# Later gating and full-height angle and magnitude matmuls in a two-layer convolution kernel

## The chip, the core and the metric

The kernel runs on one core of a Trainium2 chip. The metric is the device time of one execution in microseconds (us); the time before is the median of three executions. Engines are named as in the profile: PE (TensorE matmul), PEld (its weight load), DVE (VectorE), ACT (ScalarE), POOL (GpSimd), SP (the queue that issues most DMAs).

## The reference

Four residual layers run over a sequence of 2048 rows and 512 channels, A, B, A, B:

```
x = x + A(layernorm(x), k, v, shift_k, ssm_k, ssm_D)     # twice
x = x + B(layernorm(x), ...)                             # twice, in turn with A
A(q):  kv = shortconv4(k, shift_k) * v                   # "gating"
       y  = irfft(rfft(kv) * rfft(ssm_k)) + kv * ssm_D   # long causal convolution by FFT
       return q * y
B(u):  K[d, l] = 2 * Re sum_n C[d,n] * dt[d] * exp(A[d,n] * dt[d] * l)    # 128 modes n per channel
       return irfft(rfft(u) * rfft(K)) + u * D_skip
```

The convolution in A doesn't depend on x, so it is done once for both A layers. The taps K of layer B are made from angles (the imaginary part of A·dt times l) and magnitudes (the real part).

## The kernel before

**Stages.** A prologue works out angles and magnitudes per mode (L373 to L424, mostly DVE) and writes them, each split into a high and a low part, to the DRAM tensors `rows_d` (`split`, L359). Then two Python generators are interleaved by `run_steps`, one step of `stream` to two of `diagonal`, after four steps of `diagonal` alone. A scheduler then settles the order of instructions on each engine; every engine runs its own list strictly in order.

**`stream`** makes the taps of layer B in 65 steps (16 groups of modes, four quarters each) and, as quarters of the taps are done, their spectra. For a group, `load_rows` reads the rows back (`raw`), and one DVE cast makes `rw` of them. Its matmuls are `mags` (`pm`, L479, six per group) and `angles` (`pa`, L494, four per group, each followed by a full-height matmul `pa<-y,minus`, L499). Each group holds two halves h of 64 partitions, and each of these matmuls contracts over the 64 partitions of one half. DVE and POOL then multiply sines, cosines and magnitudes to `xye` (L517 to L519, L521), and PE contracts them (`pk`, L531).

**`diagonal`** first makes the spectra of layer A's kernel, 48 steps: per quarter four steps that load a group (`kk`), add a diagonal term on POOL (L239), transform it (`pf`, L171) and transpose it (`x`, L189), then eight steps of the second transform (`pu`, L196), the copy (`pc`) and the store (`spec`). Beside them runs the **gating** (`gated`, L622): per group of channels one load (`kvt`, 624 KB), four products on POOL (`term`, L629), a copy on ACT, three sums and a product on DVE (`acc`, `un`, L637, L639) and a store (`kv_d`). 16 groups, three generator steps each. After the spectra comes A's **convolution** (59 steps) with its loads `kab`, products `sw` and `vv`, the inverse transforms `pi` and `po` and the stores `ya_d`.

**Afterwards**, with other PSUM pools, come the first layer A's update (`gated_update`, which reads `ya_d` as `yaq`), layer B's convolution, and the second pair of layers.

Gating borrows buffers: `kvt` those of `kab`, its products those of `vv` and `sw`, its sum one of the PSUM banks of `pu`.

Of the kernel before, what the change touches and what calls it, by code (L numbers as in the profile page):

```python
# [9 lines left out]
F32 = mybir.dt.float32  # L10
F32R = mybir.dt.float32r
# [9 lines left out]
NQ = 4  # L21
CK = 4
NCH = 32 // CK
# [76 lines left out]
def kernel(ctx: ExitStack, tc: tile.TileContext, out, x_in, kv_in, ssmk_in, ssmd_in,  # L100
                           la_in, ai_in, cr_in, ci_in, ldt_in, ldtb_in, dsk_in,
                           w1_in, w2_in, mm_in, w4_in, minus_in, tt_in, tg1_in, tg2_in, dbg=None):
    nc = tc.nc
    V, S, G, T = nc.vector, nc.scalar, nc.gpsimd, nc.tensor

    def sbuf(stack, name, side="left"):
        return stack.enter_context(tc.tile_pool(name=name, bufs=1, side=side, reuse_waits="tile"))

    def after(ins, first):
        tc.add_manual_dep(ins.ins, first.ins.name,  # L110
                          mybir.DependencyInfo(mybir.DependencyClass.NoSync, mybir.DependencyReason.DATA),
                          reason="activation tables")

    dram = ctx.enter_context(tc.tile_pool(name="dram", bufs=1, space=DRAM))
# [1 line left out]
    kdram = [dram.tile([128, 512], F32, name=f"kdram{g}") for g in range(16)]  # L116
    ya_d = dram.tile([4, 128, 16, 128], F32, name="ya_d")
    kv_d = [dram.tile([128, 512], F32, name=f"kv_d{g}") for g in range(16)]
    rows_d = [dram.tile([NQ, 128, 4, 128], F32, name=f"rows_d{k}") for k in range(2)]

    cpool = sbuf(ctx, "cpool")
    GL = 2
# [295 lines left out]
    tabs = {}  # L418
# [15 lines left out]
    def stage_banks(n, wide):  # L434
        sctx.close()
        pool = sctx.enter_context(tc.tile_pool(name=f"ps{n}{wide}", bufs=1, space=PSUM, reuse_waits="tile"))
        psum["c1"] = (pool, n)
        psum.pop("f1", None)
        if wide:
            psum["f1"] = (pool, wide)  # L440
# [4 lines left out]
    wk = sbuf(gctx, "wk")  # L445
# [11 lines left out]
        factors.append(xye)  # L457


    rows, ms, pks, angs = {}, {}, {}, {}  # L460
    NM = 5
    last_exp, last_sin = [None], [None]

    def load_rows(gi):
        if gi in rows:
            return
        raw = wk.tile([128, 2, 128], F32, name="raw", tag="raw", bufs=2)
        q, g = divmod(gi, 4)
        for k in range(2):
            nc.sync.dma_start(raw[:, k, :], rows_d[k][q, :, g, :])  # L470
        rows[gi] = wk.tile([128, 2, 128], F32R, name="rw", tag="rw", bufs=2)
        V.tensor_copy(rows[gi], raw)

    def mags(gi, k, col):
        h, s = divmod(k, 2)
        hs = slice(64 * h, 64 * h + 64)
        pm = pp.tile([128, 512], F32, name="pm", tag="pa", bufs=NPA)
        rhs = tabs["tg2"][hs] if col == 2 else tabs["tg1"][hs, 8 * s:8 * s + 8, :]
        mt = T.matmul(pm, rows[gi][hs, 1, :], rhs, start=True, stop=True)  # L479
        if col == 2:  # L480
            ms[gi, h] = wk.tile([128, 16, 96], F32, name="m", tag="m", bufs=NM)
            m = ms[gi, h][:, :, 64:96]
        else:
            m = ms[gi, h][:, 8 * s:8 * s + 8, 0:64]
        i = S.activation(m, pm.rearrange("p (c i) -> p c i", c=16 if col == 2 else 8), AF.Exp)  # L485
        if last_sin[0] is not None:
            after(i, last_sin[0])
        last_exp[0] = i

    def angles(gi, k):  # L490
        h, s = divmod(k, 2)
        hs = slice(64 * h, 64 * h + 64)
        pa = pp.tile([128, 512], F32, name="pa", tag="pa", bufs=NPA)
        T.matmul(pa, rows[gi][hs, 0, :], tabs["tt"][hs, 8 * s:8 * s + 8, :], start=True, stop=False,  # L494
                 skip_group_check=True)

        y = wk.tile([128, 512], F32R, name="y", tag="y", bufs=2)
        V.tensor_scalar(y, pa, MAGIC, MAGIC, op0=ALU.add, op1=ALU.subtract)
        T.matmul(pa, minus, y, start=False, stop=True, skip_group_check=True)  # L499
        angs[gi, k] = pa  # L500
# [106 lines left out]
    def z_of_a():  # L607
        turns_z[0] += 1
        return zx[:, turns_z[0] % 2].rearrange("p (x k r) -> p x k r", k=32, r=2)

    with ExitStack() as actx:
        ap = sbuf(actx, "conv_a", "right")
        zlast = []
        ZA = 2
        NSA = 2
        NKA = 3
        ADA = 1000
        LAGA = 2
        AHA = 2
        NWA = 1  # L620

        def gated(grp):  # L622
            kvt = ap.tile([128, 39, 32], F32, name="kvt", tag="kab", bufs=NKA)
            nc.sync.dma_start(kvt.rearrange("p t c -> p (t c)"), kv_in[grp])
            tap = lambda j: kvt[:, 35 + j, :][:, None, :].to_broadcast([128, 16, 32])
            terms = []
            for j, tag in enumerate(("vv", "sw", "vv", "sw")):
                term = ap.tile([128, 16, 32], F32, name="term", tag=tag, bufs=NSA)
                G.tensor_mul(term, kvt[:, 3 - j:19 - j, :], tap(j))  # L629
                terms.append(term)  # L630
                if j == 1:
                    yield
            yield
            acc = bank("acc").rearrange("p (t c) -> p t c", c=32)
            S.copy(acc, terms[0])  # L635
            for term in terms[1:]:
                V.tensor_add(acc, acc, term)  # L637
            un = ap.tile([128, 16, 32], F32, name="un", tag="pc", bufs=2)
            V.tensor_mul(un, acc, kvt[:, 19:35, :])  # L639
            nc.sync.dma_start(kv_d[grp], un.rearrange("p t c -> p (t c)"))  # L640
            yield

        KV0 = 1
        def row_stats(t):
            xt = ap.tile([128, 512], F32, name="xt", tag="kk", bufs=3)
            nc.sync.dma_start(xt, x_in[:, t, :])
            V.bn_stats(st0[:, t, :], xt)

        def kv_steps():
            for grp in range(KV0, 16):  # L650
                yield from gated(grp)

        def steps_a(q):
            z, us = {}, {}
            nop = lambda: None

            def load(g):
                us[g] = ap.tile([128, 16, 32], F32, name="u", tag="kk", bufs=3)
                nc.sync.dma_start(us[g].rearrange("p t c -> p (t c)"), kv_d[4 * q + g])

            def fwd(g):
                if g == 0:
                    z[0] = z_of_a()
                u = us[g]
                fwd_group(lambda ps_, j, n: u[ps_, :, j:j + n], z[0], 32 * g, 32, 32 if "f1" in psum else 16, zlast[4 + q - ZA], full="f1" not in psum)
                if g < 3:
                    load(g + 1)
            turns = [lambda g=g: fwd(g) for g in range(4)]
            if LAGA > 2:
                turns = [nop, turns[0], turns[1], lambda: (turns_last[0](), turns_last[1]())]  # L670
                turns_last = [lambda: fwd(2), lambda: fwd(3)]
            return (lambda: z[0]), [nop] * 7 + [lambda: load(0)] + [nop] * 4 + turns

        def finish_a(q, g, po):
            ya = ap.tile([128, 512], F32, name="ya", tag="pc", bufs=2)
            S.copy(ya, po.rearrange("p t c -> p (t c)"))
            nc.sync.dma_start(ya_d[:, :, 4 * q + g].rearrange("k p x -> p k x"), ya.rearrange("p (k x) -> p k x", k=4))

        def diagonal():
            kvs = kv_steps()  # L680
            for q in range(NQ):
                for i, _ in enumerate(spectrum_quarter(0, q, ssmk_in, ap, zlast, ZA, "c1")):
                    if q == 0 and i == 1:
                        for grp in range(KV0):
                            for _ in gated(grp):
                                pass
                    if q == 0 and i < 4:
                        nc.sync.dma_start(w2[:, 8 * i:8 * i + 8], w2_in[:, 8 * i:8 * i + 8])
                    if q == 2 and i < 4:
                        ins = nc.sync.dma_start(mm[:, 8 * i:8 * i + 8], mm_in[:, 8 * i:8 * i + 8])  # L690
                        after(ins, zlast[0])
                    if q == 3 and i == 0:
                        after(nc.sync.dma_start(w4, w4_in), zlast[0])
                    next(kvs, 0)
                    if q == 3 or q == 2 and i >= 8:
                        row_stats(12 * (q - 2) + i - 8)
                    yield
            for _ in kvs:
                yield
            stage_banks(4, 0)  # L700
            yield from convolution(0, {"conv": ap}, steps_a, finish_a, lag=LAGA, ahead=AHA, nk=NKA, ns=NSA, nw=NWA, inplace=True,
                                   add_dve=ADA, zlast=zlast)

        RT = 1
        RD = 2
        diag = diagonal()
        for _ in range(4):
            next(diag)
        run_steps([(stream(), RT), (diag, RD)])
# [254 lines left out]
```

## Time and profile before

| what | value |
|---|---|
| median of three executions | 742.3 us (741.83, 742.3, 750.0) |
| the profiled execution's own time | 734.99 us |
| its span in the profile | 733.2 us |
| mean granted TensorE clock | 0.933 |
| PE busy | 593.9 us (81%) |
| DVE busy | 531.1 us (72%) |
| ACT busy | 486.0 us (66%) |
| POOL busy | 454.8 us (62%) |

"Busy" counts the time in which an engine runs an instruction, waits apart. The span is from the first to the last instruction. The granted clock is the share of the TensorE clock that was passed; a matmul at 0.50 takes about twice as long.

### The profile page before, as it was taken

The page shows a single profiled execution, that of the slowest core. Times are in us where ns is not written, and L with a number is a line of the kernel's source. Part 1 is how long each engine was busy: PE and PEld are TensorE (multiplying, and loading weights), DVE is VectorE, ACT ScalarE, POOL GpSimd, SP SyncE. Part 2 cuts the span into 40 slices and gives each one's busy share as a digit, 9 for nine tenths or more (in the row PEclk, how much of TensorE's full clock was granted, in tenths as well). Part 3 has the DMA queues.
Part 4 walks back from the last instruction along what each step waited for, and adds up shares of the span by engine and source line. Part 5 has one row for each costly group of instructions (what it writes and reads, how often), then busy time and mean ns, then how long its engine had stood idle before and what let it go on. Part 6 is the DMA issues. An engine that isn't in the chain of part 4 may idle for free. (4 is left out here: it accounts for less than half of the span.)

```text
span 733.2 us, 14282 instructions
## 1 busy us (share of the span) xinstructions
PE 593.9 (81%) x4984; PEld 409.9 (56%) x4984; DVE 531.1 (72%) x961; ACT 486.0 (66%) x882; POOL 454.8 (62%) x473
## 2 busy tenths in 40 slices
PE   1378877698989999969998865899798817799996
PEld 0154554456766776736765454767476503476773
DVE  7857959877385785584574877376597998978775
ACT  4246566577678777776798749677655447768672
POOL 5847969678268595684596620157576612479693
PEclk9997979768999999989999996999999978899999
DMA  9769767774745457636457493567866360178682
GB/s 324 258 227 315 255 209 235 226 249 158 223 125 143 130 127 204 167 107 173 118 149 212 136 335 150 170 181 203 226 192 164 85 172 0 51 209 238 195 244 100
DMA packets 80683, 135.39 MB, mean 185 GB/s; under 512 B 8540, under 2 KB 29412, under 8 KB 79460
## 3 DMA queue, kind: packets, MB, share of 16 engines
q1 hardware_dynamic: 79716, 132.06, 60.3%
q0 software_dynamic: 896, 2.43, 1.2%
q8 instruction: 39, 0.64, 0.4%
q14 instruction: 32, 0.26, 0.1%
HBM read 98.80 MB, written 35.65 MB: 183 GB/s over the span
## 5 line engine op out<-in xcount | busy, mean ns | idle before, releaser
L285 POOL TENSOR_TENSOR sw<-sw,kab 128x512 f32<-128x512 f32 x96 | 124.9, 1305 | 66.3 <-ACT sw L282 61.3
L283 DVE TENSOR_TENSOR vv<-pu,kab 128x512 f32<-128x512 f32 x96 | 65.1, 680 | 64.1 <-ACT sw L282 44.1
L295 PE MATMUL pi<-vv,mm 128*128 128x128 f32 x768 | 105.7, 281 | 6.7 <-DVE vv L283 4.3
L286 POOL TENSOR_TENSOR vv<-vv,sw 128x512 f32<-128x512 f32 x76 | 98.6, 1301 | 14.5 <-DVE vv L283 12.0
L295 PEld LDWEIGHTS pi<-vv,mm 128*128 128x128 f32 x768 | 94.2, 193 | 20.6 <-issue 10.4
L281 ACT ACTIVATE sw<-pu 64x512 f32<-64x512 f32 x96 | 57.1, 595 | 65.7 <-PE pu L196 61.8
L171 PE MATMUL pf<-kk,wz 128*128 128x256 f32 (+1 forms) x176 | 64.7, 624 | 42.1 <-issue 15.2
L517 POOL TENSOR_TENSOR xye<-co,m 128x512 f32<-128x512 f32 x64 | 76.0, 1187 | 36.5 <-ACT co L507 12.5
L629 POOL TENSOR_TENSOR term<-kvt 128x512 f32<-128x512 f32 x64 | 81.5, 1292 | 19.5 <-ACT acc L635 9.8
L196 PEld LDWEIGHTS pu<-zu,w 128*128 128x128 f32 x512 | 63.0, 191 | 42.8 <-DVE vv L283 16.1
L196 PE MATMUL pu<-x,w 128*128 128x128 f32 x512 | 79.6, 302 | 5.9 <-ACT pc L247 2.5
L196 PEld LDWEIGHTS pu<-x,w 128*128 128x128 f32 x512 | 70.7, 209 | 21.9 <-issue 7.5
L196 PE MATMUL pu<-zu,w 128*128 128x128 f32 x512 | 72.8, 284 | 10.7 <-DVE vv L283 9.6
L171 PE MATMUL pf<-u,wz 128*128 128x256 f32 (+2 forms) x280 | 76.4, 485 | 3.0 <-DVE zu L189 1.2
L247 ACT COPY pc<-pu 128x512 f32<-128x512 f32 x64 | 37.2, 587 | 45.3 <-PE pu L196 22.6
L485 ACT ACTIVATE m<-pm 128x512 f32<-128x512 f32 x96 | 53.4, 607 | 18.5 <-PE pm L479 15.1
L316 PE MATMUL po<-w,w 128*64 128x512 f32 x192 | 53.9, 637 | 13.8 <-DVE w L310 12.0
L171 PEld LDWEIGHTS pf<-kk,wz 128*128 128x128 f32 (+1 forms) x176 | 30.1, 222 | 58.2 <-issue 29.3
L505 ACT ACTIVATE co<-pa 128x512 f32<-128x512 f32 x64 | 38.4, 600 | 30.2 <-PE pa L499 29.8
L282 ACT COPY sw<-pu 64x512 f32<-64x512 f32 x96 | 55.5, 578 | 1.1
L518 DVE TENSOR_TENSOR xye<-pa,m 128x512 f32<-128x512 f32 x64 | 43.7, 683 | 13.8 <-ACT pa L506 7.3
L479 PE MATMUL pm<-tg,rw 64*128 64x512 f32 x96 | 43.7, 517 | 10.5 <-DVE xye L519 8.3
(137 smaller groups left out, 1147.3 us busy)
## 6 DMA issues: line engine op xcount, KB each, us to landing
kab<-spec SPq DMA_DIRECT2D x188, 256.0 KB, 4.3
spec<-pc SPq DMA_DIRECT2D x64, 256.0 KB, 2.3
kvt<-kv_in SPq DMA_DIRECT2D x16, 624.0 KB, 5.3
yaq<-ya_d SPq DMA_DIRECT2D x5, 1024.0 KB, 7.5
kk<-ssmk_in SPq DMA_DIRECT2D x16, 256.0 KB, 5.1
kv_d<-un SPq DMA_DIRECT2D x16, 256.0 KB, 4.1
xt<-x_in SPq DMA_DIRECT2D x16, 256.0 KB, 2.9
kdram<-ks SPq DMA_DIRECT2D x64, 64.0 KB, 2.9
```

Source lines behind the costliest of these rows:

```text
L171: yield T.matmul(o, w, rhs, start=True, stop=True)
L196: ins = T.matmul(pu[:, i, :], w2[:, c * CK + i, :], z[:, :, c * CK + i, :], start=True, stop=True)
L281: S.mul(sw[0:64], pu[64:128], -1.0)
L282: swapped[0] = S.copy(sw[64:128], pu[0:64])
L283: V.tensor_mul(vv, pu, kabs[s][:, 0])
L285: (V if last else G).tensor_mul(sw, sw, kabs[s][:, 1])
L286: (V if last or s % add_dve == add_dve - 1 else G).tensor_add(vv, vv, sw)
L295: i1s[t] = T.matmul(pi[:, i, :], mm[:, c * CK + i, :], vvs[t][:, i, :], start=True, stop=True)
L316: ins = T.matmul(po[64 * a:64 * a + 64], w4, ws[g][:, :, 16 * a:16 * a + 16, :].rearrange("p x t r -> p t x r"), start=True, stop=True, ti ...
L485: i = S.activation(m, pm.rearrange("p (c i) -> p c i", c=16 if col == 2 else 8), AF.Exp)
L517: G.tensor_mul(xye[:, 0, :, 32:96], co[:, :, 1:65], m[:, :, 32:96])
L629: G.tensor_mul(term, kvt[:, 3 - j:19 - j, :], tap(j))
```

## The change

Three things are done.

1. The first group's gating, which ran as a block at the second step of the spectra, goes the way of the other 15; and the gating generator is first stepped at the fourth step of the spectra (`KS = 3`) in place of the first. Its 48 steps then don't fit in the spectra, and the last three run beside the first seven steps of A's convolution.
2. `raw` becomes two fixed tiles of twice the width, [128, 2, 2, 128], zeroed once on POOL: half h of the modes stands in its own 64 partitions of slot h, the other 64 partitions of the slot stay zero. The cast to `rw` covers 128x512 elements in place of 128x256.
3. `mags` and `angles` contract over all 128 partitions of a slot; the table operand is taken whole.

```diff
+    raws = []
+    for i in range(2):
+        raw = wk.tile([128, 2, 2, 128], F32, name=f"raw{i}")
+        for h in range(2):
+            G.memset(raw[64 - 64 * h:128 - 64 * h, h], 0.0)
+        raws.append(raw)
...
-        raw = wk.tile([128, 2, 128], F32, name="raw", tag="raw", bufs=2)
+        raw = raws[gi % 2]
-        for k in range(2):
-            nc.sync.dma_start(raw[:, k, :], rows_d[k][q, :, g, :])
+        for h in range(2):
+            hs = slice(64 * h, 64 * h + 64)
+            nc.sync.dma_start(raw[hs, h], rows_d[:, q, hs, g, :].rearrange("k p n -> p k n"))
...
-        rhs = tabs["tg2"][hs] if col == 2 else tabs["tg1"][hs, 8 * s:8 * s + 8, :]
-        mt = T.matmul(pm, rows[gi][hs, 1, :], rhs, start=True, stop=True)
+        rhs = tabs["tg2"] if col == 2 else tabs["tg1"][:, 8 * s:8 * s + 8, :]
+        T.matmul(pm, rows[gi][:, h, 1, :], rhs, start=True, stop=True)
...
-        T.matmul(pa, rows[gi][hs, 0, :], tabs["tt"][hs, 8 * s:8 * s + 8, :], start=True, stop=False,
+        T.matmul(pa, rows[gi][:, h, 0, :], tabs["tt"][:, 8 * s:8 * s + 8, :], start=True, stop=False,
...
-        KV0 = 1
+        KV0 = 0
+        KS = 3
...
-                    if q == 0 and i == 1:
-                        for grp in range(KV0):
-                            for _ in gated(grp):
-                                pass
...
-                    next(kvs, 0)
+                    if 12 * q + i >= KS:
+                        next(kvs, 0)
...
+            for _ in range(NCH - 1):
+                next(kvs, 0)
+                next(main)
+                yield
```

What the scheduler makes of it moves instructions on every engine up to the first update. Three places at the start of the program show the pattern.

POOL, from the split of the magnitudes (`hl<-la`) on, before. `kk` is the addition for one group of the spectra, four of them make a quarter; `term` is a gating product:

```order
L363 TENSOR_TENSOR hl<-la,hl 128x512
L239 TENSOR_TENSOR kk<-kk,dr 1x32
L629 TENSOR_TENSOR term<-kvt 128x512 x2
L239 TENSOR_TENSOR kk<-kk,dr 1x32
L363 TENSOR_TENSOR hl<-ai,hl 128x512
L629 TENSOR_TENSOR term<-kvt 128x512 x2
L239 TENSOR_TENSOR kk<-kk,dr 1x32
L629 TENSOR_TENSOR term<-kvt 128x512 x7
L239 TENSOR_TENSOR kk<-kk,dr 1x32
L629 TENSOR_TENSOR term<-kvt 128x512
```

The same place with the change:

```order
L363 TENSOR_TENSOR hl<-la,hl 128x512
L239 TENSOR_TENSOR kk<-kk,dr 1x32 x3
L363 TENSOR_TENSOR hl<-ai,hl 128x512
L634 TENSOR_TENSOR term<-kvt 128x512 x4
L239 TENSOR_TENSOR kk<-kk,dr 1x32
```

The fourth `kk` stood behind eleven products and now stands behind four. Counted up to the first `xye` of the taps, POOL's list held 26 products and now holds 18.

SP, from the last two stores of `rows_d` to the first read of `raw`, before:

```order
L364 DMA rows_d_99<-hl 8x16x1024
L640 DMA kv_d_82<-un 128x512
L624 DMA kvt<-kv_in 128x1248
L229 DMA kk<-ssmk_in 128x512
L640 DMA kv_d_83<-un 128x512
L624 DMA kvt<-kv_in 128x1248
L226 DMA dr<-ssmd_in 1x128
L470 DMA raw<-rows_d_98 128x128
```

With the change:

```order
L364 DMA rows_d<-hl 8x16x1024 x2
L229 DMA kk<-ssmk_in 128x512
L226 DMA dr<-ssmd_in 1x128
L477 DMA raw_234<-rows_d 64x2x128 x2
L477 DMA raw_237<-rows_d 64x2x128 x2
```

Two stores of gating results and two loads of gating inputs no longer stand between.

DVE, from the last product of the prologue to the first casts, before:

```order
L363 TENSOR_TENSOR hl<-t_143,hl 128x512
L189 STREAM_TRANSPOSE x<-pf 128x512 x2
L637 TENSOR_TENSOR acc<-acc,term 128x512 x5
L639 TENSOR_TENSOR un<-acc,kvt 128x512
L637 TENSOR_TENSOR acc<-acc,term 128x512
L189 STREAM_TRANSPOSE x<-pf 128x512 x2
L639 TENSOR_TENSOR un<-acc,kvt 128x512
L189 STREAM_TRANSPOSE x<-pf 128x512 x2
L637 TENSOR_TENSOR acc<-acc,term 128x512
L472 CAST rw<-raw 128x256 x2
```

With the change:

```order
L363 TENSOR_TENSOR hl<-t_142,hl 128x512
L189 STREAM_TRANSPOSE x<-pf 128x512 x6
L479 CAST rw<-raw_234 128x512
L479 CAST rw<-raw_237 128x512
L642 TENSOR_TENSOR acc<-acc,term 128x512 x3
L644 TENSOR_TENSOR un<-acc,kvt 128x512
```

The casts now stand behind six transposes alone; the gating's sums come after them.

More of the change, by code (lines that the diff above doesn't have):

```diff
@@ L118 @@
     kv_d = [dram.tile([128, 512], F32, name=f"kv_d{g}") for g in range(16)]
-    rows_d = [dram.tile([NQ, 128, 4, 128], F32, name=f"rows_d{k}") for k in range(2)]
+    rows_d = dram.tile([2, NQ, 128, 4, 128], F32, name="rows_d")
     cpool = sbuf(ctx, "cpool")
@@ L466, in load_rows @@
             return
-        raw = wk.tile([128, 2, 128], F32, name="raw", tag="raw", bufs=2)
+        raw = raws[gi % 2]
         q, g = divmod(gi, 4)
-        for k in range(2):
-            nc.sync.dma_start(raw[:, k, :], rows_d[k][q, :, g, :])
-        rows[gi] = wk.tile([128, 2, 128], F32R, name="rw", tag="rw", bufs=2)
+        for h in range(2):
+            hs = slice(64 * h, 64 * h + 64)
+            nc.sync.dma_start(raw[hs, h], rows_d[:, q, hs, g, :].rearrange("k p n -> p k n"))
+        rows[gi] = wk.tile([128, 2, 2, 128], F32R, name="rw", tag="rw", bufs=2)
         V.tensor_copy(rows[gi], raw)
@@ L475, in mags @@
         h, s = divmod(k, 2)
-        hs = slice(64 * h, 64 * h + 64)
         pm = pp.tile([128, 512], F32, name="pm", tag="pa", bufs=NPA)
-        rhs = tabs["tg2"][hs] if col == 2 else tabs["tg1"][hs, 8 * s:8 * s + 8, :]
-        mt = T.matmul(pm, rows[gi][hs, 1, :], rhs, start=True, stop=True)
+        rhs = tabs["tg2"] if col == 2 else tabs["tg1"][:, 8 * s:8 * s + 8, :]
+        T.matmul(pm, rows[gi][:, h, 1, :], rhs, start=True, stop=True)
         if col == 2:
@@ L491, in angles @@
         h, s = divmod(k, 2)
-        hs = slice(64 * h, 64 * h + 64)
         pa = pp.tile([128, 512], F32, name="pa", tag="pa", bufs=NPA)
-        T.matmul(pa, rows[gi][hs, 0, :], tabs["tt"][hs, 8 * s:8 * s + 8, :], start=True, stop=False,
+        T.matmul(pa, rows[gi][:, h, 0, :], tabs["tt"][:, 8 * s:8 * s + 8, :], start=True, stop=False,
                  skip_group_check=True)
@@ L697, in diagonal @@
                     yield
+            stage_banks(4, 0)
+            main = convolution(0, {"conv": ap}, steps_a, finish_a, lag=LAGA, ahead=AHA, nk=NKA, ns=NSA, nw=NWA, inplace=True,
+                               add_dve=ADA, zlast=zlast)
+            for _ in range(NCH - 1):
+                next(kvs, 0)
+                next(main)
+                yield
             for _ in kvs:
                 yield
-            stage_banks(4, 0)
-            yield from convolution(0, {"conv": ap}, steps_a, finish_a, lag=LAGA, ahead=AHA, nk=NKA, ns=NSA, nw=NWA, inplace=True,
-                                   add_dve=ADA, zlast=zlast)
+            yield from main
         RT = 1
```

## The prediction

> **What bounds the kernel now.** I first read the page's parts 1 and 2 (PE busiest at 81%, its granted clock low in places), then cut the span into stages: prologue, spectra of A beside the first taps, A's convolution beside the other taps, and the rest. The view of windows gives busy time per engine (instruction counts in brackets), granted clock, DMA share and GB/s:
>
> ```profile
> 0.00:40.00 40.00, 11.37 (x20) 3.89 (x21) 30.65 (x45) 12.47 (x19) 25.77 (x36) 1.00 0.84 298
> 40.00:195.00 155.00, 128.64 (x1229) 82.92 (x1229) 115.20 (x214) 98.31 (x172) 112.66 (x121) 0.85 0.71 231
> 195.00:430.00 235.00, 211.70 (x2259) 150.69 (x2257) 156.06 (x249) 177.94 (x307) 156.13 (x160) 0.99 0.56 157
> 430.00:733.00 303.00, 242.14 (x1480) 172.43 (x1480) 229.15 (x454) 197.31 (x384) 160.27 (x156) 0.93 0.59 167
> ```
>
> The columns are PE, PEld, DVE, ACT, POOL. PE has little to do in the first 40 us. From 195 to 430 it is busy 90% at full clock: that stage is PE's, and what starts it earlier ends it earlier. From 40 to 195 no engine is full (PE 83%, DVE 74%, POOL 73%), but PE's clock is 0.85. After 430 the order of instructions is as good as unchanged, so I forecast no change there.
>
> In the prologue, timelines of POOL, PE and SP show one chain for the spectra and one for the taps. The rows give start, length, engine, line, and in brackets the idle time ahead and what ended it:
>
> ```profile
> 20.42 3.38 POOL L629 TENSOR_TENSOR term<-kvt 128x512 f32<-128x512 f32 x2
> ...
> 26.74 8.71 POOL L629 TENSOR_TENSOR term<-kvt 128x512 f32<-128x512 f32 x7 [2.29 <-ACT acc L635]
> 35.41 0.24 POOL L239 TENSOR_TENSOR kk<-kk,dr 1x32 f32<-1x32 f32 x1
> ```
> ```profile
> 35.70 2.07 PE L171 MATMUL pf<-kk,wz 64*128 64x512 f32 x2
> 39.19 3.78 PE L196 MATMUL pu<-x,w 128*128 128x128 f32 x16 [1.41 <-DVE x L189]
> ...
> 44.11 1.60 PE L479 MATMUL pm<-tg,rw 64*128 64x512 f32 x3
> ```
> ```profile
> 26.41 1.25 SPq L364 DMA_DIRECT2D rows_d<-hl  x2
> ...
> 34.47 0.38 SPq L640 DMA_DIRECT2D kv_d<-un  x1
> ...
> 35.98 3.63 SPq L470 DMA_DIRECT2D raw<-rows_d  x4
> ```
>
> The fourth `kk` of the first quarter runs on POOL only at 35.41, after the gating products ahead of it; `pf` follows at once, and the first `pu` at 39.19. The rows of angles and magnitudes are handed to DRAM at 26.41 to 27.66, but their read is issued at 35.98, behind a gating store that waited for its data until 34.47; the first `pm` starts at 44.11.
>
> The second thing to see is the clock. The first seven rows are the stretches at 0.50 up to 195 us and the stretch ahead of the longest; the last two are a later one, when PE ran nothing but `pf` of 128 rows, half of whose weights (`wz`) are zeros:
>
> ```profile
> 55.15:58.56 3.41, 3.41 (x13) 0.50 1.05 292
> 68.80:75.63 6.83, 6.83 (x48) 0.50 0.89 313
> 96.11:106.35 10.24, 9.32 (x57) 0.50 0.68 223
> 130.24:133.66 3.42, 3.42 (x10) 0.50 0.37 101
> 140.48:147.31 6.83, 3.53 (x39) 0.50 0.82 258
> 154.14:171.21 17.07, 16.24 (x102) 0.50 0.53 169
> 150.73:154.14 3.41, 3.33 (x38) 1.00 0.91 325
> 454.51:457.92 3.41, 1.59 (x8) 1.00 0.62 222
> 457.92:461.33 3.41, 2.32 (x11) 1.00 0.25 88
> ```
> ```profile
> 152.17 1.89 PE L479 MATMUL pm<-tg,rw 64*128 64x512 f32 x4
> 154.58 1.76 PE L494 MATMUL pa<-tt,rw 64*128 64x512 f32 x3 [0.51 <-ACT m L485]
> ```
> ```profile
> 453.91 2.19 PE L171 MATMUL pf<-kk,wz 128*128 128x256 f32 x8
> ```
>
> Low stretches last multiples of 3.41 us. The 3.41 us before the longest were busy for 3.33, much of it with `pm` of 64 rows, and the clock fell; 3.41 us that were busy for 1.59, with 128 rows of which half are zeros, were followed by 3.41 us at full clock. So busy time alone doesn't keep the clock: matmuls over 64 rows count less, and zeros in the array count. The six stretches are 47.8 us with 42.8 us of PE work, of which half, 21 us, is lost to the clock.
>
> **The change part by part**, against the profiled execution's own 734.99 us (span 733.2), which is 7.3 under the median of the timed runs, 742.3; I take the change in microseconds over to that median.
>
> *Earlier start.* In POOL's list of before the split of the angles stands right ahead of the products at 20.42; in the new one it is followed by four products and the fourth `kk`. Four products at the 3.38 for two of the row are 6.8: `kk` at 27.2 in place of 35.41, so 8.2 earlier. For the taps: only a small load stands between the stores of the rows and their read. The two stores are 1 MB; at the 298 GB/s of the first stage that is 3.5 us, so they land near 31.2 to 31.6, and the read goes 4.4 earlier. The cast also loses its place behind the gating's sums on DVE:
>
> ```profile
> 42.65 0.70 DVE L637 TENSOR_TENSOR acc<-acc,term 128x512 f32<-128x512 f32 x1 [3.52 <-POOL kk L239]
> 43.26 2.07 DVE L472 CAST rw<-raw 128x256 fp32r<-128x256 f32 x2
> ```
>
> ```profile
> raw<-rows_d SPq DMA_DIRECT2D x32, 64.0 KB, 1.9
> ```
>
> The data were there by 41.5 (last read issued by 39.61, 1.9 to land by the page's row of DMA issues), the cast ran at 43.26: 1.8 more, 6.2 together. Between 8.2 and 6.2 I take **-7**. The ends are -8.2 and 0 (if the four products wait as long for the gating inputs, which are now issued later).
>
> *Displaced gating.* Eight products fewer before the first `xye` must be done later:
>
> ```profile
> L629 POOL TENSOR_TENSOR term<-kvt 128x512 f32<-128x512 f32 x64 | 81.5, 1292 | 19.5 <-ACT acc L635 9.8 <-DVE acc L637 7.1 <-DMA kvt<-kv_in 2.3
> ```
>
> Eight by 1.29 are 10.3 us of POOL. Four of them go past the spectra, where PE is the bound and POOL busy 66%: 0. The other four, 5.2 us, fall into 40 to 195, where POOL is busy 73%; I take half, **+2.6**. The ends are 0 and +10.3. Behind a product wait its sum on ACT and DVE and, since the sum holds one of two PSUM banks, the next `pu`.
>
> *The clock.* With 128 rows, the stretch before 154.14 counts in full, and the clock should hold there; PE then saves half of 16.24, 8.1 us. But the others are near their own limits there:
>
> ```profile
> 150.00:160.00 10.00, 9.09 (x58) 5.58 (x57) 7.96 (x13) 6.67 (x14) 8.65 (x8) 0.71 0.76 251
> 160.00:170.00 10.00, 10.00 (x57) 6.08 (x56) 7.39 (x14) 6.64 (x12) 8.21 (x11) 0.50 0.49 166
> 170.00:180.00 10.00, 8.47 (x126) 6.46 (x129) 6.66 (x13) 8.69 (x16) 8.14 (x10) 0.94 0.59 193
> ```
>
> POOL has 5.0 us free in these 30, so at most that much can be had before it is the bound: **-4**. The other five stretches begin after PE stood idle, which 128 rows don't cure; some would end one step of 3.41 sooner. I put 0 on them. The ends for the whole are 0 and -10.5 (all of the 21 us lost, half of it on the path).
>
> [...]
>
> *Length of the matmuls themselves.* Rows of 64 and 128 of the same 512 columns:
>
> ```profile
> L479 PE MATMUL pm<-tg,rw 64*128 64x512 f32 x96 | 43.7, 517 | 10.5 <-DVE xye L519 8.3 <-ACT m L485 1.7
> L499 PE MATMUL pa<-y,minus 128*128 128x512 f32 x64 | 31.2, 514 | 1.2 <-DVE y L498 0.8
> ```
>
> A full one (514 ns) is no longer than a half one. But two halves can run beside each other:
>
> ```profile
> 148.76 0.73 PE L479 MATMUL pm<-tg,rw 64*128 64x512 f32 x2
> ...
> 108.14 0.98 PE L479 MATMUL pm<-tg,rw 64*128 64x512 f32 x2
> ```
>
> Two took 0.73 in one place, 0.98 in another. If the 0.25 is overlap of opposite halves and it is lost at each of at most 32 changes of half (two per group), it is 8 us of PE; as few rows show it, and part lies where PE waits, I take **+1**, with ends 0 and +8.
>
> [...]
>
> *Casts, memsets, reads.* The 16 casts double in width; a cast of 512 elements took 0.41 in the prologue, the fastest of 256 took 0.28, so 16 by 0.13 are 2.1 us of DVE, mostly beside PE: **+0.5**.
>
> ```profile
> 13.97 0.41 DVE L406 CAST t<-e_i 128x512 f32<-128x512 int32 x1
> ```
> ```profile
> L472 DVE CAST rw<-raw x16: 282/624/6206, 43.3 to 375.0; 128x256 fp32r<-128x256 f32 x16
> ```
> ```profile
> 319.91 6.21 DVE L472 CAST rw<-raw 128x256 fp32r<-128x256 f32 x1
> ```
>
> Half of the casts took 0.62 or less, but the one at 319.91 stood for 6.2 us. The trace doesn't say how often the new ones will; 0, with ends -6.2 and +6.2. The four memsets are bounded by the one of 128x256 elements in the prologue, 0.31 each; by the new order they stand behind the fourth `kk`, off both chains: 0, at most +1.2. The reads of `raw` keep their count and bytes: 0.
>
> ```profile
> 0.77 0.31 POOL L347 MEMSET wz<- 128x256 f32 x1
> ```
>
> **Sum:** -7 + 2.6 - 4 + 1 + 0.5 = -6.9, so 728.1 by the profiled execution and **735.4** by the median.
>
> **The rivals.** *More than that:* stream and spectra both gain the 8.2, the displaced products all find gaps, the clock gives 8.1 and the 6.2 us cast is not repeated: -22 at most, -14 as a middle, so 728 and down to 720. For it speaks that each of the four has its row; against it, that POOL has only 42 us free in 155 and must take both the products and the quicker taps. *No gain:* the four products wait for `kvt`, whose first load is now issued later, and the lost overlap of halves costs some 4 while the clock gives 4: 742, between 739 and 746. For it: DMA ran at 0.84 of its time in the first stage. *Slower, POOL as the bound:* if the stretch from 40 to 195 is POOL's once the taps come sooner, the earlier start gives nothing, the clock gives nothing, and the eight products and memsets are paid in full, 10.3 + 1.2, with 2 for the casts: +13.5, 756. It decides once less than 11.5 of POOL's 42 idle us lie where a product has its inputs; in the stretches of 10 us shown POOL is busy 81 to 87%, which speaks for it, the mean of 73% against it.
>
> **How the numbers follow.** My forecast, 729 to 740, has 0.50; more than that 0.24; no gain 0.17; slower 0.09. Two per cent, 14.8 us, is about what can be told from no change here. Below 727.5 lies most of the second case: 0.23 for faster. Above 757.1 lies under half of the last: 0.04 for slower. The rest, 0.73, is within. The range from 720 to 747 leaves out the far ends of the second and last case.
>
> **What would show it.** In the changed profile the fourth `kk` near 27 and the first `pm` near 37 show the start; `term` beside `sw` only in the first steps of the convolution; no stretch at 0.50 that begins while PE is busy with `pm` or `pa`; rows of `pm` and `pa` as 128*128 at 510 to 540 ns; and the last `ya_d` some 7 us earlier. I am wrong if POOL's busy share from 40 to 195 rises over 85%, if a cast stands for 5 us again on the path, or if the clock falls as before in busy stretches.

## The result, and the profile after

| | before | after |
|---|---|---|
| median of 20 executions each | 741.75 us | 742.44 us |
| the profiled execution's own time, its span | 734.99, 733.2 us | 739.65, 737.5 us |
| mean granted clock | 0.933 | 0.911 |
| time at 0.50 between 40 and 195 us | 47.8 us | 60.5 us |

The ratio is 1.0095, 95% interval 1.0066 to 1.0124: no gain, and if anything a loss. Executions of one kernel scatter here by 2 to 3% (before: 729 to 750 but for one of 854), and the ratio compares only those near each kernel's fastest, so the medians of all executions on one chip stand beside every ratio below, and the clock is not read from the profiles of e5, e7, e9 and e10, whose executions lay at the slow end of theirs.

The view of windows after, in the stages of before (PE, PEld, DVE, ACT, POOL, clock, DMA share, GB/s):

```profile
0.00:40.00 40.00, 14.25 (x38) 6.85 (x39) 26.40 (x41) 13.12 (x20) 17.55 (x34) 1.00 0.75 271
40.00:195.00 155.00, 117.82 (x1049) 73.88 (x1047) 118.84 (x206) 90.56 (x157) 112.06 (x115) 0.80 0.65 210
195.00:430.00 235.00, 213.26 (x2260) 159.98 (x2260) 148.06 (x244) 180.77 (x314) 162.43 (x166) 0.94 0.57 161
430.00:738.00 308.00, 252.40 (x1639) 179.74 (x1639) 239.39 (x473) 201.15 (x391) 165.54 (x164) 0.93 0.62 176
```

From 40 to 195 PE did 1049 matmuls where it had done 1229, at a clock of 0.80 for 0.85. POOL worked 112.06 us there, as good as the 112.66 of before, although more was asked of it. From 195 to 430 the clock was 0.94 for 0.99: 28.3 us at 0.50, where before had 6.8.

The start did move. Timelines of POOL, SP and PE after:

```profile
22.55 5.83 POOL L634 TENSOR_TENSOR term<-kvt 128x512 f32<-128x512 f32 x4 [2.18 <-DMA kvt<-kv_in]
28.34 0.24 POOL L239 TENSOR_TENSOR kk<-kk,dr 1x32 f32<-1x32 f32 x1
...
34.21 0.67 POOL L464 MEMSET raw<- 64x256 f32 x2 [4.73 <-DMA rows_d<-hl]
```
```profile
34.23 2.64 SPq L477 DMA_DIRECT2D raw<-rows_d  x4
```
```profile
34.38 3.78 PE L196 MATMUL pu<-x,w 128*128 128x128 f32 x16 [1.42 <-DVE x L189]
38.10 1.54 PE L171 MATMUL pf<-kk,wz 64*128 64x512 f32 x4
39.57 0.96 PE L485 MATMUL pm<-tg,rw 128*128 128x512 f32 x3
```

The fourth `kk` runs 7.1 us earlier (28.34 for 35.41), the first `pu` 4.8, the first `pm` 4.5, the first `xye` 4.4. Counted in POOL's and PE's timelines, this is what had been started at four times, before / after:

| | 40 us | 112 us | 170 us | 195 us |
|---|---|---|---|---|
| gating products (of 64) | 12 / 4 | 41 / 34 | 63 / 50 | 64 / 60 |
| `xye` of the taps (of 128) | 0 / 0 | 16 / 16 | 36 / 36 | 48 / 44 |
| `kk` of the spectra (of 16, then of B's) | 4 / 6 | 16 / 16 | 20 / 20 | 21 / 20 |

At 112 us taps and spectra stand where they stood, and seven products are owed. One place where the lead of the taps goes can be seen on POOL. After the fifth and sixth `xye` four products now run in a row, where before two did (after, then before), and the lead of 4.2 us at the fifth `xye` is 1.8 us at the seventh:

```profile
74.90 4.96 POOL L634 TENSOR_TENSOR term<-kvt 128x512 f32<-128x512 f32 x4
```
```profile
79.11 2.50 POOL L629 TENSOR_TENSOR term<-kvt 128x512 f32<-128x512 f32 x2
```

The rest is paid from there: the last `pu` of A's spectra comes 15.7 us later than before, the last product 33.5, the first `sw` of the convolution 19.1. Of this the convolution, the update and the second layer give back all but 4.3 at the end of the profiled span.

What was said of the length of single matmuls holds, and what was said of the casts doesn't:

```profile
L485 PE MATMUL pm<-tg,rw 128*128 128x512 f32 x96 | 43.1, 516 | 11.4 <-ACT m L491 7.7 <-DVE xye L524 3.5
L504 PE MATMUL pa<-y,minus 128*128 128x512 f32 x64 | 31.5, 507 | 10.4 <-DVE y L503 10.3
L479 DVE CAST rw<-raw 128x512 fp32r<-128x512 f32 x16 | 21.9, 1371 | 3.9 <-DMA raw<-rows_d 3.9
```

DVE, POOL and PE around the longest cast:

```profile
168.61 0.68 DVE L503 TENSOR_SCALAR y<-pa 128x512 fp32r<-128x512 f32 x1
169.20 7.16 DVE L479 CAST rw<-raw 128x512 fp32r<-128x512 f32 x1
176.28 0.68 DVE L503 TENSOR_SCALAR y<-pa 128x512 fp32r<-128x512 f32 x1
```
```profile
168.81 1.16 POOL L522 TENSOR_TENSOR xye<-co,m 128x512 f32<-128x512 f32 x1
169.94 0.68 POOL L526 TENSOR_TENSOR xye<-co,m 128x256 f32<-128x256 f32 x1
170.59 3.72 POOL L634 TENSOR_TENSOR term<-kvt 128x512 f32<-128x512 f32 x3
174.28 1.16 POOL L522 TENSOR_TENSOR xye<-co,m 128x512 f32<-128x512 f32 x1
175.41 0.67 POOL L526 TENSOR_TENSOR xye<-co,m 128x256 f32<-128x256 f32 x1
177.64 1.27 POOL L634 TENSOR_TENSOR term<-kvt 128x512 f32<-128x512 f32 x1 [1.57 <-DVE acc L642]
```
```profile
172.52 1.12 PE L171 MATMUL pf<-kk,wz 64*128 64x512 f32 x2
177.01 0.79 PE L504 MATMUL pa<-y,minus 128*128 128x512 f32 x1 [3.37 <-DVE y L503]
```

The fastest cast took 0.40. This one ends (at 176.36) just after an unbroken run of seven POOL instructions ends (176.08), and PE stands 3.37 us for the `y` behind it. Another of 3.64 us at 122.75 lies beside four unbroken `xye` in the same way.

### The profile page after: what moved, and what is told of

Its sections match the earlier page's. It is cut to its first block, busy times and chain, and to the rows that moved or that the text cites. A ratio compares the mean times of both kernels' runs of the same rounds, so it can differ in the third digit from the quotient of the medians.

```text
span 737.5 us, 14292 instructions
## 1 busy us (share of the span) xinstructions
PE 597.7 (81%) x4984; PEld 420.4 (57%) x4984; DVE 532.7 (72%) x961; ACT 485.6 (66%) x882; POOL 457.6 (62%) x477
## 5 line engine op out<-in xcount | busy, mean ns | idle before, releaser
L286 POOL TENSOR_TENSOR vv<-vv,sw 128x512 f32<-128x512 f32 x76 | 99.0, 1306 | 12.6 <-DVE vv L283 10.0
L171 PE MATMUL pf<-kk,wz 128*128 128x256 f32 (+1 forms) x176 | 60.8, 595 | 39.4 <-issue 13.2
L196 PE MATMUL pu<-x,w 128*128 128x128 f32 x512 | 82.5, 311 | 9.4 <-ACT pc L247 4.1
L196 PEld LDWEIGHTS pu<-x,w 128*128 128x128 f32 x512 | 76.2, 221 | 22.2 <-ACT pc L247 7.1
L171 PE MATMUL pf<-u,wz 128*128 128x256 f32 (+2 forms) x280 | 78.9, 495 | 3.5 <-ACT pc L247 1.5
L171 PEld LDWEIGHTS pf<-kk,wz 128*128 128x128 f32 (+1 forms) x176 | 27.5, 214 | 55.5 <-issue 29.3
L536 PEld LDWEIGHTS pk<-xye 128*32 128x32 f32 x2048 | 38.0, 119 | 33.1 <-issue 20.4
L536 PE MATMUL pk<-xye 128*32 128x64 f32 x2048 | 53.5, 238 | 3.6 <-POOL xye L526 3.5
```

The costliest lines, as they stand in the source:

```text
L171: yield T.matmul(o, w, rhs, start=True, stop=True)
L196: ins = T.matmul(pu[:, i, :], w2[:, c * CK + i, :], z[:, :, c * CK + i, :], start=True, stop=True)
L286: (V if last or s % add_dve == add_dve - 1 else G).tensor_add(vv, vv, sw)
L536: T.matmul(pk[32 * i4:32 * i4 + 32, 2 * k + i, :], xye[:, r, 4 * i + i4, 64:96], xye[:, r, 4 * i + i4, 0:64], start=r == 0, stop=r == 1, t ...
```

## The experiments

Differences in the text are of medians, kernel less before on the same chip; the interval of the ratio stands in brackets.

**The parts alone.** Theories: *L*, the late gating eats its own gain; *C*, the casts that are held up eat it. e1 is part 1 of the diff on its own:

```diff
-        KV0 = 1
+        KV0 = 0
+        KS = 3
```

> Part 1 of the change alone; rows, casts and the matmuls of angles and magnitudes as before (narrow casts, 64 rows). Theory L (the late gating eats its own gain: its products come 11 to 34 us later from 110 us on, behind sums on ACT and DVE, and the spectra end late): ratio 1.003 to 1.010, first product of the convolution (sw) 10 to 20 us later than in the kernel before though the fourth kk stays 7 us earlier. Theory C (the doubled casts, blocked on DVE while POOL runs, eat the gain of the earlier start): without them the gain stays, ratio 0.990 to 0.995, first sw not later than before.

Measured: 755.81, +14.9; ratio 1.0267 (1.0201 to 1.0333). The fourth `kk` is 7.8 us earlier and the first `sw` 22.0 later. L has the direction, yet the loss is larger than it said. The clock between 40 and 195:

```profile
40.00:195.00 155.00, 122.58 (x976) 78.44 (x974) 108.46 (x196) 82.61 (x144) 105.03 (x108) 0.71 0.63 206
```

90.1 us at 0.50, where before had 47.8. e2 is parts 2 and 3 of the diff (`raws`, the wide cast, the whole tables) on their own:

```diff
+        T.matmul(pm, rows[gi][:, h, 1, :], rhs, start=True, stop=True)
```

> Parts 2 and 3 alone (zeroed double-width tiles, casts of 128x512, matmuls over 128 rows); gating as before. Theory L: ratio 0.990 to 1.000, since the start is that of before and the clock's low stretches shrink by 5 to 15 us between 40 and 195 us. Theory C: ratio 1.003 to 1.010, with one or two casts of 3 us or more between 40 and 195 us that PE waits for. A third, that the rows do nothing at all for the clock: as many us at 0.50 between 40 and 195 as before (47.8), ratio 0.998 to 1.003.

Measured: 736.72, -4.2; ratio 1.0006 (0.9963 to 1.005), so by the ratio no difference; 37.5 us at 0.50, ten fewer than before, which speaks against the third theory and for L, although the ratio itself lies in the third theory's range. Two casts took 3.31 and 4.14 us there, as C said, and yet it is no slower.

**Without the casts.** The rows go from DRAM straight into tiles of the matmuls' type:

```diff
-        rows[gi] = wk.tile([128, 2, 2, 128], F32R, name="rw", tag="rw", bufs=2)
-        V.tensor_copy(rows[gi], raw)
+        rows[gi] = raw          # raws: four F32R tiles, filled through .bitcast(F32)
...
-                        load_rows(gi + 1)
+                        load_rows(gi + 2)
```

> The whole change, but the rows are read from DRAM straight into four tiles of the matmuls' type and the 16 casts on DVE are gone; a read is issued one group earlier. Theory C: the 3.6 and 7.2 us of two blocked casts go off the path, 6 to 11 us faster than the changed kernel, ratio to before 0.985 to 0.995. Theory L: the casts are only where DVE happens to wait, ratio 1.003 to 1.010 as for the change.

> The kernel before, with nothing changed but that its 16 casts of 128x256 go, the rows read straight into four tiles of the matmuls' type, one group earlier. Theory C: before had a cast of 6.2 us at 320, where PE is the bound, and none above 3 us ahead of it; ratio 0.992 to 1.000. Theory L has no term for it: 0.997 to 1.003.

Measured: e3 726.6, -14.3; 0.9876 (0.9835 to 0.9918). e4 739.41, -1.5; 1.0069 (1.0025 to 1.0112). C holds for e3; e4 is outside what either said. Casts seemed to matter only in the changed kernel. But the scheduler gives every one of these kernels another order of instructions, and that is a second difference between them.

**One order held.** So from here a kernel gets a list of instructions per engine, taken from another kernel, and every instruction is made to follow the one ahead of it in that list (an order alone, no wait):

```diff
+    for names in ORDER.values():
...
+        for a, b in zip(names, names[1:]):
+            tc.add_manual_dep(insts[f"I-{b}"], f"I-{a}",
```

Each row of the table at the end of this part names the order that a kernel had. e5 is the change with `rows[gi][hs, h, 1, :]` and the tables cut by `hs` again, e6 the change less its casts with reads at their old place, e7 parts 2 and 3 in the order of before, e8 the change in the order of e1.

> The changed kernel, with every engine's list of instructions held in the changed kernel's order; its matmuls pm and pa alone contract over the 64 partitions of their half again (tiles, zeros, casts and reads stay wide). Theory T (a half clock holds itself: at 0.50 a PE that is busy all the time with 64-row matmuls doesn't get its clock back, with 128 rows it does): 80 to 100 us at 0.50 between 40 and 195 us, as with gating alone (90), where the change had 60; ratio 1.015 to 1.03. Theory O (rows mean little; kernels differ by the order that the scheduler gave them): 55 to 65 us at 0.50, ratio 1.003 to 1.012, as the change.

> The changed kernel in its own order, less the 16 casts: the rows are read straight into four tiles of the matmuls' type, each read at its old place in SP's list (not one group earlier). Theory C (casts blocked on DVE stood on the path with 3.6 and 7.2 us, and PE's clock fell behind them): 6 to 16 us faster than the change, ratio 0.985 to 0.998. Theory O (the kernel without casts gained by its other order and earlier reads): ratio 1.002 to 1.012.

> The kernel before in its own order, with parts 2 and 3 of the change (wide zeroed tiles, casts of 128x512, 128 rows). Theory T: fewer us at 0.50 between 40 and 195 than before's 48, 30 to 40, and no window of 3.41 us in which PE is busy over 90% and the clock stays at 0.50 (before has four); ratio 0.990 to 0.998. Theory O: 44 to 52 us at 0.50, ratio 0.998 to 1.004.

> The whole change, held in the order that the scheduler gave to gating alone. Theory T: 45 to 65 us at 0.50 between 40 and 195 where gating alone had 90, and 12 to 20 us faster than it (755.8): ratio 1.000 to 1.008. Theory O: the time of gating alone, ratio 1.02 to 1.03.

Measured: e5 750.34, +11.4; 1.0158 (1.0081 to 1.0234). e6 731.05, -7.9; 0.9908 (0.9857 to 0.9958). e7 736.84, -2.1; 0.9944 (0.9867 to 1.002). e8 748.62, +9.7; 1.0156 (1.0084 to 1.0229). What e5 and e7 were to show of the time at 0.50 stays open; e7's interval reaches into the ranges of both theories.

*Rows count* (T, against O): with nothing else changed, 64 rows cost the changed kernel about 10 us by the medians. The intervals of the two ratios overlap (1.0081 to 1.0234 for e5, 1.0066 to 1.0124 for the change); the clearest pair is e15 and e16 below. How rows count, e1 and e8 show in one order; the windows of 3.41 us of e1 (64 rows), then e8 (128) at the same work:

```profile
102.56:105.97 3.41, 3.41 (x10) 1.91 (x9) 0.88 (x2) 0.00 (x0) 0.00 (x0) 0.50 1.00 372
105.97:109.39 3.42, 3.42 (x12) 2.35 (x11) 0.62 (x1) 2.16 (x4) 0.88 (x2) 0.50 0.32 121
109.39:112.80 3.41, 3.41 (x34) 1.73 (x35) 0.77 (x2) 1.78 (x3) 3.08 (x3) 0.50 0.22 77
112.80:116.21 3.41, 2.69 (x11) 1.25 (x10) 2.70 (x5) 2.05 (x4) 2.19 (x2) 0.50 0.17 44
116.21:119.63 3.42, 3.42 (x8) 1.54 (x8) 3.42 (x7) 0.61 (x2) 1.58 (x2) 0.50 0.35 90
```
```profile
104.31:107.73 3.42, 3.42 (x12) 2.59 (x12) 0.39 (x2) 0.62 (x2) 0.00 (x0) 0.50 0.76 290
107.73:111.14 3.41, 3.41 (x45) 2.29 (x44) 1.71 (x3) 3.41 (x8) 2.13 (x3) 1.00 0.39 145
```

e1's PE is busy all the time for three windows, and the clock stays at 0.50. The second of them (105.97) and e8's first (104.31) hold much the same work, eight `pu`, two `pm` and the end of what ran before; e8's `pm` have 128 rows, and its clock is back after that one window. In e1's third window `pm` of 64 rows run between `pk`, which uses 32 columns:

```profile
109.42 0.79 PE L479 MATMUL pm<-tg,rw 64*128 64x512 f32 x1
110.15 0.87 PE L531 MATMUL pk<-xye 128*32 128x64 f32 x24
110.94 0.79 PE L479 MATMUL pm<-tg,rw 64*128 64x512 f32 x1
```

But e8 still has 78.0 us at 0.50, more than the 45 to 65 that T gave, and is 5.2 us faster than e1 for T's 12 to 20: T is right on what these windows show and more than twice too large, since stretches also begin where PE waits (e8's that ends at 107.73 began at 100.90, after a window in which PE was busy for 1.60 of 3.41 us). O keeps a part: e8 and the change differ in nothing but order, and by 8.5 us (the intervals of their ratios overlap).

*Casts* (e6): 9.0 us better than the change (+1.2 on its own repeat, below). Up to the 17th `xye` e6 runs as the changed kernel (120.17 and 119.49 us); at the 49th it is 11.3 us ahead, and stays 11 to 14 ahead to the end. The two casts in that stretch took 3.64 and 7.16, together 10.8, and its lead jumps by 3.4 and by 5.0 us where they stood. In e6 the `y` follows the one ahead of it at once, and the same `pa<-y` (the 21st), which had waited 3.37, doesn't wait:

```profile
165.04 1.28 DVE L502 TENSOR_SCALAR y<-pa 128x512 fp32r<-128x512 f32 x2
```
```profile
168.66 0.50 PE L503 MATMUL pa<-y,minus 128*128 128x512 f32 x1
```

**The old gating, 64 rows and a later gating, without casts; the change again.** e9 is e3 with `KV0 = 1` and the block of before, in the order that the scheduler gives it; e10 e3's order with 64 rows, e11 e3 with

```diff
-        KS = 3
+        KS = 6
```

and e12 the changed kernel itself.

> 128 rows and no casts as in the whole change without casts (726.6 us on its chip, 14.3 under before), but gating at its old place. With both disturbers gone, theory S (the early start is worth what was forecast for it, 7 less 2.6, once nothing eats it) has this kernel 3 to 8 us over the whole change without casts: ratio 0.990 to 1.000. Theory L (the late gating costs more than its start brings, whatever the casts and rows): this kernel is as fast as that one or faster, ratio 0.980 to 0.988.

> The whole change without casts (reads one group early), every engine's list held in its order, pm and pa over 64 partitions again. Theory T: the clock is lost as in the two kernels with 64 rows and late gating, 60 to 90 us at 0.50 between 40 and 195 where it had 30.7; 8 to 15 us slower than it, ratio 0.995 to 1.010. If rows matter only where casts have stopped PE: 30 to 40 us at 0.50, ratio 0.985 to 0.992.

> The whole change without casts, gating first stepped at the seventh step of the spectra (KS = 6) in place of the fourth; six of its steps run beside the convolution. Theory S: the start gains again, since the fourth kk and more of the spectra stand ahead of all products: 2 to 6 us faster than with KS = 3, ratio 0.980 to 0.986. Theory L: the products pushed back again end the spectra later, 3 us slower or more, ratio 0.991 to 1.000.

> The changed kernel itself, for a comparison on one chip with the three beside it. All theories: as timed, 0 to 2 us over before by the medians, ratio 1.000 to 1.012, with 50 to 65 us at 0.50 between 40 and 195 us and one or two casts of 3 us or more there.

Measured: e9 740.12, -0.7; 0.9978 (0.9932 to 1.0024). e10 738.2, -2.7; 0.9957 (0.9904 to 1.0009). e11 726.5, -14.4; 0.9805 (0.9756 to 0.9853). e12 742.04, +1.2; 1.0061 (1.0008 to 1.0114). e10 is rows again: 12 us in one order, with a ratio that lies in T's range. e9 against e3 speaks for S, and more strongly than S asked: the late gating would bring 13.6 us. But e9's order is its own, and e14 below, with the same edits but for the earlier reads, in the order of before, is 14 us faster. e11's ratio lies in S's range and its median, on another chip, is e3's; L is out, a further gain not settled.

**The orders of before and of gating alone, without casts.** e13 and e14 stand in the order of before (64 and 128 rows), e15 and e16 in the order of e1; the edits are those above. Theory X: casts and 64 rows cost little until the late gating makes PE wait.

> The kernel before in its own order (gating at its old place, 64 rows), less the 16 casts, each read at its old place. Theory X (casts and 64 rows cost little until the late gating makes PE wait): within 4 us of before, ratio 0.994 to 1.004. Theory C alone (a cast costs wherever it stands): 6 to 10 us faster, as in the change's order, ratio 0.985 to 0.993.

> The kernel before in its own order with 128 rows and without casts; gating at its old place. Theory X: 2 to 6 us faster than before (the rows gave 2.1 in this order), ratio 0.990 to 0.998. If the gain of the best kernels (14 us) comes from rows and casts and not from the gating: ratio 0.978 to 0.986.

> Gating alone in its own order (64 rows), less the 16 casts. With casts it was 14.9 us slower than before. Theory X: the casts are a third to two thirds of that loss, ratio 1.004 to 1.013. Theory O (the order that the late gating got is bad by itself): ratio 1.015 to 1.025. If the casts are all of it: ratio 0.985 to 1.000.

> The whole change without casts, in the order of gating alone, 128 rows. With casts it was 9.7 us slower than before. Theory X: casts and rows together take back most of the loss, and the early start shows: ratio 0.985 to 0.998. Theory O: still slower than before, ratio 1.005 to 1.013.

Measured: e13 730.09, -9.9; 0.9887 (0.9848 to 0.9925). e14 725.28, -14.7; 0.9835 (0.9791 to 0.9879). e15 740.57, +0.6; 0.9998 (0.9954 to 1.0042). e16 727.86, -12.1; 0.9879 (0.9825 to 0.9934). X falls with e13 and e14, although e16 is in its range: the casts cost 9.9 us in the order of before, 12.6 at 128 rows, and 14.3 and 21.8 in the order of e1, where at 64 rows they were all of the loss against before (e15). Which of the 16 casts the gain comes from, no run separates. And the best kernels' 14 us come from rows and casts, not from the gating (e14). Rows again: e15's and e16's windows from 85 to 112 and from 112 to 195, 64 rows and then 128 in one order.

```profile
85.00:112.00 27.00, 22.49 (x176) 12.68 (x177) 16.32 (x33) 14.00 (x25) 15.67 (x17) 0.61 0.51 160
112.00:195.00 83.00, 67.92 (x667) 45.12 (x667) 60.39 (x116) 50.93 (x89) 60.99 (x63) 0.76 0.63 206
```
```profile
85.00:112.00 27.00, 22.00 (x222) 12.48 (x220) 17.52 (x35) 14.88 (x27) 17.34 (x19) 0.81 0.57 189
112.00:195.00 83.00, 62.45 (x669) 41.49 (x667) 63.00 (x120) 51.81 (x90) 62.86 (x66) 0.84 0.67 213
```

**By what the casts cost.** The 16 casts become maxima of the tile with itself, in the same place and with the same result, in the change's order (e17) and in before's (e18):

```diff
-        V.tensor_copy(rows[gi], raw)
+        V.tensor_max(rows[gi], raw, raw)
```

> The changed kernel in its own order; each of the 16 casts is a maximum of the tile with itself (two input streams) in the same place of DVE's list, with the same result. Theory B (the one-input cast is held up while POOL runs, for 3.6 and 7.2 us in two places; an operation with two inputs isn't): all 16 take 0.5 to 0.9 us, none over 1.5; 5 to 9 us faster than the change, near the kernel without casts in this order, ratio 0.989 to 0.998. Theory P (the place in DVE's list costs, behind the reads and ahead of PE's inputs, whatever the operation): ratio 1.001 to 1.012, as the change.

> The kernel before in its own order, its 16 casts as maxima of the tile with itself. Theory B: all take 0.3 to 0.6 us; 6 to 10 us faster than before, as without casts in this order, ratio 0.986 to 0.994. Theory P: within 3 us of before, ratio 0.997 to 1.003.

Measured: e17 741.98, +0.7; 1.0051 (1.0007 to 1.0094). e18 735.39, -5.9; 0.9939 (0.9891 to 0.9988). In e17 three of the 16 maxima stand for 3.92, 7.03 and 4.19 us. The longest stands as long as the cast had, again to the end of POOL's run (175.96 + 0.67 = 176.63; the maximum ends at 177.18):

```profile
170.15 7.03 DVE L479 TENSOR_TENSOR rw<-raw 128x512 fp32r<-128x512 f32 x1
```
```profile
175.96 0.67 POOL L526 TENSOR_TENSOR xye<-co,m 128x256 f32<-128x256 f32 x1
178.46 1.28 POOL L634 TENSOR_TENSOR term<-kvt 128x512 f32<-128x512 f32 x1 [1.84 <-DVE acc L642]
```

In e18 the one that had stood 6.21 us in before took 1.01: it ended at 322.62, just after an `xye` of POOL's (322.34), while the `sw` behind that had begun (322.31); another, at 92.56, stood 2.82 us, as the cast there had in before (2.24):

```profile
321.61 1.01 DVE L472 TENSOR_TENSOR rw<-raw 128x256 fp32r<-128x256 f32 x1
```

Theory B, that two inputs are free of the hold, is wrong by e17 (7.03 us, through seven POOL instructions in a row). Theory P, that the place costs whatever the operation, doesn't fit e18, where the place was the same and 5.2 us of standing went, although the interval of e18's ratio just reaches P's range. That the hold is POOL's run is what the timelines show of all 23 casts or maxima of over 2 us, in ten profiles: POOL was busy for 86% or more of each, through an unbroken run of three to seven instructions, and each ended 0.1 to 0.6 us after that run did. Why the maximum at 321 was done so soon and the one at 170 was not stays open.

All kernels but e17 and e18, median less that of before on the same chip, in us (us at 0.50 between 40 and 195 in brackets where read):

| gating, order held | 64 rows, casts | 128 rows, casts | 64 rows, no casts | 128 rows, no casts |
|---|---|---|---|---|
| old; before's | 0 (47.8) | e7 -2.1 | e13 -9.9 (58.0) | e14 -14.7 (54.6) |
| late; that of e1 | e1 +14.9 (90.1) | e8 +9.7 (78.0) | e15 +0.6 (75.1) | e16 -12.1 (51.2) |
| late; the change's | e5 +11.4 | change +0.7, e12 +1.2 (60.5, 62.5) | not tried | e6 -7.9 (44.4) |
| late; e3's, reads a group earlier | | | e10 -2.7 | e3 -14.3 (30.7) |
| late (KS = 6); its own, reads a group earlier | | | | e11 -14.4 (37.5) |
| old; their own, e4 and e9 with reads a group earlier | | e2 -4.2 (37.5) | e4 -1.5 (51.2) | e9 -0.7 |

The intervals of the ratios are 2 to 6 us to either side, so two cells that differ by less than some 6 us can't be told apart. Down each column the gating part can be read at equal rows and casts, against the order of before: +14.9 and +11.4; +11.8 and about +3; +10.5 and +7.2; +2.6, +6.8, +0.4 and +0.3. Late gating gained in none of them; in the last column only e6's 6.8 is more than can be told from nothing. Nor does the time at 0.50 alone rank the kernels: e13 and e14 have more of it than before and are 9.9 and 14.7 us faster. e14, with the old gating, 725.28 us, is as good as any, and beats both kernels; e3, e11 and e16 come near it with the late one.

## Why the prediction was wrong, point by point

The forecast was 7 us faster; it came out 0.7 (and 1.2 on the repeat) slower. In the table the way from before to the change has two steps, rows and then gating: -2.1 and +2.8 (+3.2 on the repeat). The prediction's terms for these two were -4 + 1 + 0.5 = -2.5 and -7 + 2.6 = -4.4. The second is the one that failed. Taken the other way, in the change's order, gating comes first with +11.4 (e5) and the rows then take back 10 to 11: again gating has the wrong sign. That the first step met its -2.5 is partly luck, since what rows are worth hangs on the order.

- **Earlier start, -7: the step that failed.** The chains did start 7.1 and 4.5 us earlier. (The reads went at 34.23, not at 31.6: the stores landed later, and two memsets of POOL waited 4.73 us with them.) The step took it as given that an earlier start arrives at the end. It had gone by 112 us, as the table of counts shows: same taps, same spectra, seven products fewer. Of the 4.2 us of the taps 2.4 went where four products ran between two pairs of `xye` (74.90).
- **Displaced gating, +2.6: mis-sized, with the start.** I let POOL's 42 idle us hide half of the products moved into 40 to 195. POOL did 112.06 us of work there for 112.66: it hid none of them. Its idle time is waits, of the products above all:

```profile
POOL term L629 <- ACT acc L635: 7.5, 3, 4.4
```
```profile
POOL term L634 <- ACT acc L640: 11.4, 5, 4.7
```

  (85 to 200 us, before and after: us, times, longest. Together with the products' waits for DVE's sums these are 14.0 and 16.2 us.) The product behind which POOL waits stands in one list with `xye` and `kk`. That this list is what makes the late gating costly fits the counts and the waits; no run took the products away, so it is argued, not shown. Nor does a run separate the move itself from the order that the scheduler then chose.
- **The clock, -4.** Rows do count, and more than I gave them where gating is late: 10, 12 and 13 us in the three pairs e5, e10 and e15, 5 in e1 and e8; 2 and 5 with the old gating, each too little to be told from nothing by itself. The part of the mechanism that I forecast came: none of the changed kernel's nine stretches at 0.50 between 40 and 195 begins in busy work any more (PE was busy for 2.01 us or less of the 3.41 ahead of each, where before's longest came after 3.33). The time at 0.50 rose all the same, since new stretches begin where PE waits: the five that "begin after PE stood idle" I had put at 0, but not what would add to them. That busy time alone doesn't decide, e1's rows show too: busy for 3.41 of 3.41 at 0.50 and still at 0.50 after.
- **Lost overlap of halves, +1.** About the size, by rows that I misread. Two full-height `pm` also take 0.72 us (at 39.57), so the 0.73 against 0.98 was not overlap. Opposite halves that do run at once stand elsewhere in before: nine pairs of `pm` or `pa` start within 0.01 us of each other, and three `pm` with such a pair take 0.74 us where three full-height ones take 0.96 (39.57). By estimate, nine times 0.22 are 2.0 us of PE.

```profile
336.99 0.74 PE L479 MATMUL pm<-tg,rw 64*128 64x512 f32 x3
```

- **Casts, +0.5 and 0 with ends of 6.2: far too small.** Holding-up was put down as a matter of one cast, here or there. The casts are worth 9 to 22 us in every order held, and were so in before, where 9.9 us had been there to be had. In the difference between the two kernels it nearly cancels (12.6 us without casts in before's order at 128 rows, 9.0 in the change's).
- **Memsets and reads, 0.** As said of their cost, but for the 4.73 us of waiting, which lies where POOL had nothing else ready (the load that the next `kk` needs landed at 34.81).
- **What would prove it wrong** named three things: POOL over 85% from 40 to 195 (it was 72%), a cast of 5 us on the path (7.16), the clock falling as before in busy stretches. The cast alone came: the time at 0.50 rose to 60.5 us, but in stretches that begin after waits. The rival *no gain* gave 739 to 746 and so has the time, but by other means: the wait for `kvt` held the fourth `kk` up by 1.1 us only (28.34 for the 27.2 forecast), and the lost overlap is some 2 us and not 4. The rival *POOL as the bound* had the right engine and the right condition, that few of its idle us lie where a product has its inputs, at a chance of 0.09; the sign that was to tell it, a busy share over 85%, was the wrong one. That its 756 is what gating alone took (755.8) is a coincidence: that kernel has 64 rows and casts of 256 elements.

## What to carry to other kernels

Idle time of an engine that runs one list strictly in order hides work only if it comes when that work has its inputs; here POOL's 42 idle us hid none (112.06 us of work for 112.66). So count what an engine has started at a few times, not its busy share. Before an edit is judged by its time, hold every engine's order: the same kernel in two orders came out 8.5 us apart (e8 against e12), and 14 us apart where reads also moved (e9 against e14), more than the edit. And look for an instruction whose duration jumps from 0.4 to 7 us beside another engine's unbroken run: taking it out was worth more than moving work around it.

## What the runs showed of the hardware

- Held up by POOL: a DVE cast of 128x512, of which the fastest took 0.40 us, stood 7.16 us, to the end of seven unbroken POOL instructions; a two-input maximum in its place 7.03. All 23 that stood over 2 us ended within 0.6 us of the end of such a run.
- The clock: eight `pu` took 2.07 us at 0.50 (before, 156.27) and 1.05 at 1.00 (243.06). Windows of 3.41 us that are busy throughout didn't bring 1.00 back where `pm` of 64 rows ran beside `pu` (e1, 105.97 to 109.39) or beside `pk` of 32 columns (109.39 to 112.80). At one order and without casts, 128 rows cut the time at 0.50 from 75.1 to 51.2 us and the kernel by 12.7 us, though half of the rows are zeros. What the columns of `pk` had to do with it, no run tested.
